# The first three groups on the window of the later ones: 168 keys per 64 tokens, one pair of bias tables, other loads

## The chip, the cores and the metric

One core of a Trainium2 chip runs one program. The metric is device microseconds of one execution; lower is better. PE is the matmul engine TensorE, DVE is VectorE, ACT is ScalarE, POOL is GpSimd; SP only issues transfers. Each engine works through its own queue in order and waits at an instruction until the semaphores of that instruction are there.

## What is computed

Attention with a local window and eight global keys, over 4 batches, 8 heads, 768 tokens and 64 features per head; its output is the input of a two-layer network with an ELU between the layers. The heart of the reference:

```python
keep = (pos[None, :] < n_global) | ((rel >= 0) & (rel < n_local))   # rel = query position - key position
scores = scale * q @ k.T - slopes * dist                            # dist = rel, or n_local for a far global key
a = softmax(where(keep, scores, -1e9))
x = (a @ v) as 3072 rows of 512
h = x @ w_in                                                        # 512 -> 2048
out = where(h > 0, h, exp(min(h, 0)) - 1) @ w_out                   # 2048 -> 512
```

Here `n_global` is 8 and `n_local` is 96. All sums are float32 or finer; `w_in` and `w_out` arrive as float64.

## The kernel before, in words

The 3072 tokens are 12 **groups** of 256 tokens (two tiles of 128). The network's hidden width is cut into 16 pieces, `fc` 0 to 15. A group needs, for each piece, the up product `h` (`mm1`, 12 matmuls of 256 columns: the high and low halves of the weight times the high part of x, then the high half times the low part `xl`), five elementwise steps, and the down product `o` (`mm2`, 6 matmuls of 512 columns). Each of the 32 weight pieces comes once, 512 KB of float64 bits (`bits`), and `weight` turns it into two fp32r halves: one ACT step, three to four DVE steps on `g`, one copy, and one subtraction on POOL.

Attention is done per group and pair of heads, so four **pairs** per group. The last nine groups use `far` and `turned`: 64 queries see 168 keys (96 before, 32, the 8 global ones, 32), the probabilities are turned by DVE and two transfers through DRAM. The first three groups, twelve pairs, use `pair` and `heads32` instead, in plain float32: scores of 128 queries against 256 keys (`s`, one tile; the very first tile of the sequence has 128 keys only), bias and maximum on DVE (`L451`), exponent on ACT (`L453`), 1/sum on DVE, the division (`norm`) on any of three engines, four transposes per tile on PE (`t`), copies to SBUF (`pt`), and the product with the values (`pv`). `xh` and `xl` are the high and low part of the result. `rqv` holds queries and values of a pair and is loaded before `rk`, its keys.

The two kinds of attention have bias tables of their own: `tab0`/`tab1` (256 wide) are made in `setup`, `far0`/`far1` (168 wide) later by `face`, on POOL.

Nothing is ordered by hand. `Plan.add` collects every step with alternatives of engine, an assumed cost and a due time; `Plan.order` walks a list schedule over them, picks engine and buffer slot, and the instructions are written out in that order. The network's pieces of the first three groups go in four segments (`SEGS`): pieces 0 to 3 for groups 0, 1 and 2, then 4 to 7 for the three, and so on. Until the first up product `warm` puts filler matmuls (`none<-fill`, `L930`) where the plan sees PE idle. The buffers of the weight pieces 12 to 15 serve the first pairs (`FIRST`, `EARLY`), so these weights are loaded only after all pairs.

Of the kernel before, what the change touches and what calls it, by code (L numbers as in the profile page):

```python
# [34 lines left out]
KW = P + NT * (NG + P)  # L35
KS = BACKW + NT * KN
VC = 2 * NT * P

# [169 lines left out]
def pe(cols):  # L208
    return (("PE", cols * 0.47, False),)
# [37 lines left out]
class Kernel:  # L247
# [64 lines left out]
    def consts(self):  # L312
        self.ident = self.const("ident", [P, P])
        self.tab0, self.tab1 = self.const("tab0", [P, P]), self.const("tab1", [P, 2 * P])
# [7 lines left out]
    def setup(self):  # L322
# [20 lines left out]
        tab0, tab1 = self.tab0.t, self.tab1.t  # L343
        nnl = self.c.tile([P, 1], F32, name="nnl")
        ii = m.tile([P, 2 * P], I32, tag="io0", name="ii")
        d = m.tile([P, 2 * P], F32, tag="io1", name="d")
        j = self.c.tile([P, NG], I32, name="tabj")
        g = self.c.tile([P, NG], F32, name="tabg")
        after = m.tile([P, P], F32, tag="io2", name="after")

        nc.gpsimd.iota(ii[:, P:], pattern=[[-1, P]], base=0, channel_multiplier=1)
        nc.gpsimd.iota(ii[:, :P], pattern=[[-1, P]], base=NL, channel_multiplier=1)
# [11 lines left out]
        nc.vector.tensor_tensor(tab0, tab1[:, P:], d[:, P:], ALU.add)  # L364
        nc.vector.tensor_scalar(g, g, nnl, None, ALU.add)
        nc.vector.tensor_copy(tab1[:, P:], tab0)
        nc.vector.tensor_tensor(tab0[:, :NG], tab0[:, :NG], g, ALU.max)
        nc.vector.tensor_tensor(tab1[:, :NL], tab1[:, :NL], d[:, :NL], ALU.add)
        nc.vector.tensor_copy(tab1[:, NL:P], g)
        self.g = g  # L370


    def weight(self, which, fc, due, after):
# [20 lines left out]
        p.add(act(DM) + pool(DM, False), lambda e: self.copy(e, w.t[:, HI], gf()), [g], [w], due - 3000)  # L394
# [16 lines left out]
    def pair(self, b, gi, hp, xh, xl, due, step, X):  # L411
        nc, p = self.nc, self.plan
        t0 = gi * NT
        nq, nk = W, KW
        rqv = self.sb("rqv", "rqv", [P, nq + VC], slots=X.get("rqv"))
        rk = self.sb("rk", "rk", [P, nk], slots=X.get("rk"))
# [9 lines left out]
        p.add(act(W) + dve(W, True) + (("POOL", 60 + 1.1 * W, True),), lambda e: self.scaled(e, q32()[:, 0], q32()[:, 0], sc), [rqv], [rqv], due - 9000)  # L426
        pv = self.bank("pv", "pv", [P, NT, P], X.get("pv"))
        for tiles in (range(NT),) if X.get("whole") else ((i,) for i in range(NT)):
            self.heads32(b, hp, t0, tiles, q32, k32, v32, rqv, rk, pv, due - 2 * step, 2 * step, X)
# [3 lines left out]
        if "pr" in X:  # L433
            self.held += [o for v in (rqv, rk) for o in v.readers]
# [8 lines left out]
    def softmax(self, b, h, t, s, m, pr, st, i, d):  # L443

        nc, p = self.nc, self.plan
        lo = 0 if t else P
        n = 2 * P - lo
        at = (b * self.H + h) * (self.S // P) + t
        nm = self.nmax.t[:, at:at + 1]
        tab = self.tab1.t if t else self.tab0.t  # L450
# [19 lines left out]
    def heads32(self, b, hp, t0, tiles, q32, k32, v32, rqv, rk, pv, due, step, X):  # L470
# [6 lines left out]
        n = {i: 2 * P - lo[i] for i in tiles}  # L477
        pts = {}

        def scores(e):  # L480
            for m, i in enumerate(tiles):
                c0 = NG + i * (NG + P) + lo[i]
                for r, s in zip(rows, ss):
# [672 lines left out]
```

## Time and profile before

| what | us |
|---|---|
| median of 3 runs | 660.91 (660.63 to 661.07) |
| the profiled execution | 661.28 |
| its span, first to last instruction | 659.4 |

The profiled execution lies 0.37 above the median, and 1.88 of it lie outside the span. A row of the timeline gives start, duration, engine, line, operation, output and inputs, and in brackets the idle time ahead of it with what ended it. Durations of neighbours on DVE and ACT overlap by some hundredths to a tenth of a microsecond; on PE the next start tells more than the duration.

### The profile page before, as it was taken

To read this page: it belongs to the slowest core of one execution; us is meant where nothing else is said; L and a number is where in the kernel's file an instruction comes from. 1 tells how busy PE (TensorE), PEld (TensorE's weight loads), DVE (VectorE), ACT (ScalarE), POOL (GpSimd) and SP (SyncE) were. 2 spreads that over 40 slices of the span, in tenths; PEclk is the share of its full clock that TensorE was granted. 3 is DMA by queue.
4 is the path that set the end of the run, shared out by engine and by line. 5 is a ranking of instruction groups with operands and counts; after the bars stand their busy time and mean duration, and the time that the engine had idled before them with its cause. 6 is when DMAs were issued, how large, how long until landed. Compare 5 with 4: busy or idle time off the path is not lost.

```text
span 659.4 us, 15420 instructions
## 1 busy us (share of the span) xinstructions
PE 647.1 (98%) x5584; PEld 564.0 (86%) x5584; DVE 386.2 (59%) x1287; ACT 403.4 (61%) x1209; POOL 150.1 (23%) x420
## 2 busy tenths in 40 slices
PE   8989999999999999999999999999999999999996
PEld 5767788898888888889889889889888888888995
DVE  6999879888664563563553554564554454443232
ACT  6999867665654664664664665655565565554442
POOL 3665654554220220220210111121121121110000
PEclk9999999999999999999999999999999999999999
DMA  7994273200263452462453354344245264030001
GB/s 306 401 407 158 80 279 98 55 2 1 70 196 101 121 148 82 120 166 83 120 140 108 107 134 128 96 128 136 71 142 142 65 163 132 34 96 1 34 1 34
DMA packets 67185, 80.55 MB, mean 122 GB/s; under 512 B 6048, under 2 KB 49312, under 8 KB 67104
## 3 DMA queue, kind: packets, MB, share of 16 engines
q1 hardware_dynamic: 66816, 79.39, 38.7%
q8 instruction: 45, 0.74, 0.5%
q14 instruction: 36, 0.29, 0.2%
q10 hardware_dynamic: 288, 0.13, 0.1%
HBM read 59.05 MB, written 20.45 MB: 121 GB/s over the span
## 4 chain that ended last, share of the span: by engine, by line
PE 83%; DVE 5%; DMA 4%; ACT 3%; issue 2%; POOL 1%; SPq 1%; POOLq 0%; DVEq 0%; ACTq 0%
PE o L752 37%; PE h L730 37%; PE pv L616 4%; PE s L544 3%; DMA bits<-in_w_out_dram 1%; DMA rqv<-in_qkv_dram 1%; DVE g L390 1%; DMA bits<-in_w_in_dram 1%; DMA pt<-dd 1%; PE t L512 1%; DVE g L388 1%; PE pv L490 1%; POOL w L309 1%; DVE g L392 1%; PE s L484 0%
## 5 line engine op out<-in xcount | busy, mean ns | idle before, releaser
L730 PEld LDWEIGHTS h<-xh,w 128*128 128x128 f32 x1536 | 233.6, 188 | 31.2 <-issue 1.1
L752 PE MATMUL o<-w,gh 128*128 128x512 f32 x768 | 243.5, 400 | 1.2 <-ACT gh L301 1.1
L730 PE MATMUL h<-xh,w 128*128 128x256 f32 x1536 | 243.6, 282 | 0.3 <-DVE gl L309 0.2
L738 DVE SCALAR_TENSOR_TENSOR h<-e,h 128x256 f32<-128x256 f32 x192 | 82.0, 427 | 175.1 <-ACT e L737 174.9
L752 PEld LDWEIGHTS o<-w,gh 128*128 128x128 f32 x768 | 129.9, 189 | 25.7 <-ACT gh L301 5.5
L736 ACT ACTIVATE e<-h 128x256 f32<-128x256 f32 x192 | 73.9, 385 | 125.0 <-PE h L730 124.5
L580 POOL TENSOR_SCALAR pr<-pr,st 128x168 f32<-128x168 f32 x144 | 58.3, 405 | 368.4 <-DVE st L461 248.1
L752 PE MATMUL o<-w,gl 128*128 128x512 f32 x384 | 128.0, 396 | 0.0
L730 PE MATMUL h<-xl,w 128*128 128x256 f32 x768 | 120.7, 279 | 0.1
L301 ACT CAST gh<-h 128x256 fp32r<-128x256 f32 x192 | 71.4, 372 | 67.0 <-DVE h L738 65.4
L309 DVE TENSOR_TENSOR gl<-h,gh 128x256 fp32r<-128x256 f32 x192 | 80.2, 418 | 45.7 <-ACT gh L301 45.4
L730 PEld LDWEIGHTS h<-xl,w 128*128 128x128 f32 x768 | 102.8, 188 | 0.5 <-DVE xl L309 0.3
L737 ACT ACTIVATE e<-e 128x256 f32<-128x256 f32 x192 | 79.9, 416 | 4.6
L572 ACT ACTIVATE pr<-pr,nmax 128x168 f32<-128x168 f32 x144 | 61.5, 427 | 20.4 <-DVE nmax L570 20.4
L752 PEld LDWEIGHTS o<-w,gl 128*128 128x128 f32 x384 | 61.8, 188 | 2.8 <-issue 0.8
L585 DVE STREAM_TRANSPOSE tr<-pr 128x192 f32<-128x192 f32 x144 | 48.0, 360 | 1.8 <-POOL pr L580 0.6
L309 POOL TENSOR_TENSOR w<-g,w 128x512 fp32r<-128x512 f32 x32 | 42.8, 1346 | 20.7 <-ACT w L301 17.8
L570 DVE CUSTOM_DVE_ANT_0 pr<-s,far 128x168 f32<-128x168 f32 x144 | 39.2, 327 | 11.9 <-PE s L544 11.9
L616 PEld LDWEIGHTS pv<-pt,v 64*64 64x64 f32 x1152 | 27.5, 133 | 8.7 <-PE h L730 5.8
L616 PE MATMUL pv<-pt,v 64*64 64x64 f32 (+1 forms) x1152 | 32.4, 250 | 0.2 <-DMA pt<-dd 0.2
L309 DVE TENSOR_TENSOR xl<-pv,xh 128x256 fp32r<-128x256 f32 x48 | 20.3, 423 | 17.1 <-ACT xh L301 15.9
L544 PE MATMUL s<-qk 64*64 64x168 f32 x576 | 27.3, 304 | 0.0
(101 smaller groups left out, 518.7 us busy)
## 6 DMA issues: line engine op xcount, KB each, us to landing
dd<-tr SPq DMA_DIRECT2D x72, 192.0 KB, 2.8
qk<-in_qkv_dram SPq DMA_DIRECT2D x36, 312.0 KB, 3.1
v<-in_qkv_dram SPq DMA_DIRECT2D x36, 256.0 KB, 3.5
pt<-dd SPq DMA_DIRECT2D x72, 128.0 KB, 2.9
bits<-in_w_in_dram SPq DMA_DIRECT2D x16, 512.0 KB, 8.0
bits<-in_w_out_dram SPq DMA_DIRECT2D x16, 512.0 KB, 8.8
out_dram<-ob SPq DMA_DIRECT2D x23, 256.0 KB, 2.1
rqv<-in_qkv_dram SPq DMA_DIRECT2D x12, 384.0 KB, 6.6
```

The source lines that it names most:

```text
L301: self.nc.scalar.copy(out, x)
L309: self.on(e).tensor_tensor(out, x, y, ALU.subtract)
L544: nc.tensor.matmul(ss[j].t[r * HW:(r + 1) * HW, i, :LW], q()[g, i * P + r * HW:i * P + (r + 1) * HW], k()[g, i * KN + r * HW:i * KN + r * ...
L572: p.add(act(LW, extra=200), lambda e, pr=pr, i=i, j=j, nm=nm: nc.scalar.activation(pr.t[:, :LW], pr.t[:, :LW], AF.Exp, bias=nm, scale=-1.0 ...
L580: nc.gpsimd.tensor_scalar(pr.t[:, :LW], pr.t[:, :LW], st.t[:, n, 3:4], 1.0, ALU.mult, ALU.mult)
L585: nc.vector.transpose(tr.t[:, :, j, i], pr.t.rearrange("p (b r) -> p b r", r=32))
L616: self.nc.tensor.matmul(pv[g].t[j * 64:j * 64 + 64, i].rearrange("p (q r) -> p q r", q=4)[:, q], vv[rows, 2 * i + a, j], pt.t[rows, q, a, ...
L730: nc.tensor.matmul(h.t, w1.t[:, s, cc * P:(cc + 1) * P], x.t[:, cc], start=n == 0 and cc == 0, stop=n == 2 and cc == self.NCC - 1)
L736: p.add(act(W, True), lambda e: nc.scalar.activation(ex.t, h.t, AF.Relu, scale=-1.0), [h], [ex], d - 8000)
L737: p.add(act(W), lambda e: nc.scalar.activation(ex.t, ex.t, AF.Exp, scale=-1.0), [ex], [ex], d - 8000)
L738: p.add(dve(W), lambda e: nc.vector.scalar_tensor_tensor(h.t, ex.t, -1.0, h.t, ALU.add, ALU.max), [h, ex], [h], d - 8000)
L752: nc.tensor.matmul(acc[i].t, g.t[:, i * P:(i + 1) * P], w2.t[:, s], start=fc == f0 and n == 0 and s == HI, stop=fc == f1 - 1 and n == 1)
```

## The change

`pair` and `heads32` use the layout of the later groups: per tile eight small score matmuls (two halves of 64 queries, two heads, 168 keys) through a function that `far` now shares, one 168-wide bias, exponent and division per head and tile, transposes of two pieces of 84 keys, and value products of 84 keys by 64 queries, twice as many and half as wide. `face` and the 256-wide tables go; `far0` and `far1` are made in `setup`, where ACT now copies three times. A pair loads `qk` (312 KB) and then `v` (84 partitions of 4 KB, 336 KB). Three numbers of the plan change too (assumed matmul cost, the spacing `NEXT` of the pairs of groups 1 and 2, the slot lists), and the high half of a weight may be copied by DVE.

```diff
-KW = P + NT * (NG + P)
+CW = LW // 2
+VN = 4 * NT * P
...
-    return (("PE", cols * 0.47, False),)
+    return (("PE", cols * 0.458, False),)
...
+        nc.scalar.copy(far0, far1)
...
+        nc.vector.tensor_tensor(far1, far1, d, ALU.add)
+        for r, at in halves:
+            nc.scalar.copy(far1[r, at:at + NG], g[r])
...
-        p.add(act(DM) + pool(DM, False), lambda e: self.copy(e, w.t[:, HI], gf()), [g], [w], due - 3000)
+        p.add(act(DM) + pool(DM, False) + dve(DM, True), lambda e: self.copy(e, w.t[:, HI], gf()), [g], [w], due - 3000)
...
-        loads = [p.add(sp(), lambda e: nc.sync.dma_start(rqv.t, src[:, :nq + VC]), writes=[rqv], due=due - 9000, nbytes=P * (nq + VC) * 4)]
-        loads += [p.add(sp(), lambda e: nc.sync.dma_start(rk.t, src[:, nq + VC:]), writes=[rk], due=due - 9000, nbytes=P * nk * 4)]
+        loads = [p.add(sp(), lambda e: nc.sync.dma_start(qk.t, src[:, :W + KS]), writes=[qk], due=due - 9000, nbytes=P * (W + KS) * 4)]
+        loads += [p.add(sp(), lambda e: nc.sync.dma_start(v.t[:CW], src[:CW, W + KS:]), writes=[v], due=due - 9000, nbytes=CW * VN * 4)]
...
+    def scores(self, qk, ss, tiles):
+        q, k = qk.t[:, :W], qk.t[:, W:]
+        for m, i in enumerate(tiles):
+            for r in range(2):
+                for j in range(2):
+                    g = slice(j * HW, (j + 1) * HW)
+                    self.nc.tensor.matmul(ss[j].t[r * HW:(r + 1) * HW, m, :LW], q[g, i * P + r * HW:i * P + (r + 1) * HW],
+                                          k[g, i * KN + r * HW:i * KN + r * HW + LW], start=True, stop=True)
...
-                for a in range(lo[i] // P, 2):
-                    for j in range(2):
-                        nc.tensor.matmul(pv.t[rows[j], i], v32()[:, 2 * i + a, j], pts[i].t[:, j, a], start=a == lo[i] // P, stop=a == 1)
+                for r in range(2):
+                    x = slice(r * HW, (r + 1) * HW)
+                    for a in range(2):
+                        for j in range(2):
+                            nc.tensor.matmul(pv.t[rows[j], i, x], vv[:CW, i, r, a, j], pts[i].t[:CW, j, a, x], start=a == 0, stop=a == 1)
...
-                        nc.tensor.transpose(tp.t[:, j, a], prs[j].t[:, a * P:(a + 1) * P], self.ident.t)
+                        nc.tensor.transpose(tp.t[:CW, j, a], prs[j].t[:, a * CW:(a + 1) * CW], self.ident.t)
...
-    def face(self, due):
...
-    NEXT = 8000.0
+    NEXT = 6000.0
```

How the queues move is seen at two places. The first is the head of ACT's queue. `rqv_153` and `qk_158` are the queries of the first pair, `far_70` and `far_71` are `far0` and `far1`, `tabg` holds the bias of the global keys. Before:

```order
L231 DMA n_raw<-in_n_dram 128x4
L331 ACT_TABLE_LOAD
L331 ACTIVATE act<-act 128x1
L437 ACTIVATE rqv_153<-rqv_153,scale 128x256
L453 ACTIVATE pr_195,st_74<-pr_195,nmax 128x128
```

And with the change:

```order
L232 DMA n_raw<-in_n_dram 128x4
L332 ACT_TABLE_LOAD
L332 ACTIVATE act<-act 128x1
L361 COPY far_70<-far_71 128x168
L377 COPY far_71<-tabg 64x8 x2
L440 ACTIVATE qk_158<-qk_158,scale 128x256
L455 ACTIVATE pr_204,st_74<-pr_204,nmax 128x168
```

The scaling of the first queries now stands behind table copies, the last of which need the finished tables of DVE.

The second place is PE where the last of the twelve pairs ends and group 2 begins. `pv_1269` and `pv_1368` are the last value products, `h_1298` and `h_1403` the first up product of group 2, an `o` a down product (`gh` and `gl` are its inputs). Before:

```order
L490 MATMUL pv_1269<-pt_1229,rqv_761 64x128 x4
L490 MATMUL pv_1269<-pt_1249,rqv_761 64x128 x4
L730 MATMUL h_1298<-xh_1005,w_78_338 128x256 x8
L730 MATMUL h_1298<-xl_1017,w_78_338 128x256 x4
L730 MATMUL h_1322<-xh_1005,w_84_447 128x256 x8
L730 MATMUL h_1322<-xl_1017,w_84_447 128x256 x4
L752 MATMUL o_1370<-w_81_580,gh_1361 128x512 x2
```

With the change:

```order
L497 MATMUL pv_1368<-pt_1327,v_833 64x64 x8
L497 MATMUL pv_1368<-pt_1355,v_833 64x64 x8
L700 MATMUL o_1248<-w_93_1064,gh_1339 128x512 x2
L700 MATMUL o_1305<-w_93_1064,gh_1339 128x512 x2
L678 MATMUL h_1403<-xh_1086,w_78_498 128x256 x8
L678 MATMUL h_1403<-xl_1096,w_78_498 128x256 x4
L700 MATMUL o_1248<-w_93_1064,gl_1346 128x512
L700 MATMUL o_1305<-w_93_1064,gl_1346 128x512
L700 MATMUL o_1248<-w_99_1174,gh_1399 128x512 x2
L678 MATMUL h_1442<-xh_1086,w_84_594 128x256 x4
```

Two pieces of group 1's down product, twelve matmuls, that stood ahead of the last pair now stand behind it, between the up products of group 2. The eight score matmuls of the first `far` pair, ahead of it too, also moved behind. Ahead of the last bias instruction of the twelve pairs, DVE's queue holds 21 `L390`/`L392` and 16 `L387`/`L388` steps on weights before, and 18 and 12 with the change, plus 4 copies of high halves; 13 divisions and query scalings stand there in both, ten of the divisions 256 wide before and 168 now; 14 elementwise steps of the network before, 10 now; 9 `pt` copies of 256 and 5 of 128 columns before, 14 of 256 now.

## Rows read from the trace of the kernel before

**Rows 1.** The page, part 1: busy us (share of the span), instructions.

```profile
PE 647.1 (98%) x5584; PEld 564.0 (86%) x5584; DVE 386.2 (59%) x1287; ACT 403.4 (61%) x1209; POOL 150.1 (23%) x420
```

**Rows 2.** Stretches: length; PE, PEld, DVE, ACT, POOL busy; clock; DMA share; GB/s.

```profile
15.00:20.00 5.00, 5.00 (x37) 3.03 (x34) 4.70 (x22) 4.81 (x16) 3.32 (x6) 1.00 1.03 401
50.00:60.00 10.00, 9.60 (x83) 7.28 (x82) 9.93 (x33) 9.00 (x29) 4.64 (x6) 1.00 0.59 217
80.00:90.00 10.00, 8.78 (x58) 7.81 (x57) 7.25 (x20) 6.65 (x19) 6.10 (x12) 1.00 1.00 372
```

**Rows 3.** Timeline of PE: first scores, first up product, end of the pairs.

```profile
6.73 0.93 PE L484 MATMUL s<-rk,rqv 64*128 64x128 f32 x8 [0.41 <-ACT rqv L437]
...
28.65 1.64 PE L730 MATMUL h<-xh,w 128*128 128x256 f32 x12
...
78.25 1.56 PE L730 MATMUL h<-xh,w 128*128 128x256 f32 x8
...
80.48 1.11 PE L730 MATMUL h<-xh,w 128*128 128x256 f32 x8
...
83.19 1.21 PE L752 MATMUL o<-w,gh 128*128 128x512 f32 x4 [1.13 <-ACT gh L301]
```

**Rows 4.** Timeline of DVE and ACT: constants, first scaling, first and last bias.

```profile
5.63 0.17 DVE L239 CAST n_f<-n_raw 128x4 f32<-128x4 int32 x1 [1.02 <-DMA n_raw<-in_n_dram]
...
7.89 0.29 DVE L451 CUSTOM_DVE_ANT_0 pr<-s,tab 128x128 f32<-128x128 f32 x1
...
70.33 0.42 DVE L451 CUSTOM_DVE_ANT_0 pr<-s,tab 128x256 f32<-128x256 f32 x1
...
6.15 0.51 ACT L437 ACTIVATE rqv<-rqv,scale 128x256 f32<-128x256 f32 x1 [3.39 <-DMA rqv<-in_qkv_dram]
```

**Rows 5.** DVE groups by shape, 0 to 80 us: busy us, mean ns.

```profile
L451 DVE CUSTOM_DVE_ANT_0 pr<-s,tab 128x256 f32<-128x256 f32 x40 | 15.9, 415 | 1.5 <-PE t L512 1.4
L390 DVE SCALAR_TENSOR_TENSOR g<-bits,g 128x512 int32<-128x512 int32 x12 | 8.3, 700 | 0.0
L388 DVE TENSOR_SCALAR g<-g 128x512 int32<-128x512 int32 x13 | 6.5, 518 | 0.0
...
L451 DVE CUSTOM_DVE_ANT_0 pr<-s,tab 128x128 f32<-128x128 f32 x8 | 2.2, 280 | 0.0
...
L570 DVE CUSTOM_DVE_ANT_0 pr<-s,far 128x168 f32<-128x168 f32 x4 | 1.1, 330 | 0.7 <-PE s L544 0.7
```

**Rows 6.** Timeline of PE: a first-group pair, then a `far` visit.

```profile
45.29 1.13 PE L484 MATMUL s<-rk,rqv 64*128 64x256 f32 x8
46.35 1.09 PE L490 MATMUL pv<-pt,rqv 128*64 128x128 f32 x16
47.38 0.74 PE L730 MATMUL h<-xh,w 128*128 128x256 f32 x4
...
108.33 0.90 PE L616 MATMUL pv<-pt,v 64*64 64x128 f32 x32
109.05 0.75 PE L544 MATMUL s<-qk 64*64 64x168 f32 x16
109.73 0.50 PE L752 MATMUL o<-w,gl 128*128 128x512 f32 x1
```

**Rows 7.** Chain that ended last: start us, us, what.

```profile
144.06 0.94 PE h L730 x8
145.00 1.17 PE o L752 x5
```

**Rows 8.** Loads of the page, part 6: KB each, median us to landing.

```profile
rqv<-in_qkv_dram SPq DMA_DIRECT2D x12, 384.0 KB, 6.6
...
rk<-in_qkv_dram SPq DMA_DIRECT2D x12, 200.0 KB, 6.6
```

**Rows 9.** Last weight of pieces 4 to 7: its low half, its first use.

```profile
97.19 1.30 POOL L309 TENSOR_TENSOR w<-g,w 128x512 fp32r<-128x512 f32 x1 [2.13 <-ACT w L301]
...
101.50 0.62 PE L752 MATMUL o<-w,gh 128*128 128x512 f32 x2
```

More of the change, by code (lines that the diff above doesn't have):

```diff
@@ L433, in pair @@
         if "pr" in X:
-            self.held += [o for v in (rqv, rk) for o in v.readers]
+            self.held += qk.readers + v.readers
     def scaled(self, e, out, x, sc):
@@ L463, in inverse, with norm, heads32 @@
         self.plan.add((("DVE", 290.0, False),), inverse, [st], [st], due, slack=slack)
-    def norm(self, pr, lo, st, i, due, both):
-        n = 2 * P - lo
-        return self.plan.add((act(n, extra=90) if both else ()) + (("DVE", 130 + 0.53 * n, True), ("POOL", 60 + 1.1 * n, True)), lambda e: self.scaled(
-            e, pr.t[:, lo:], pr.t[:, lo:], st.t[:, i, 3:4]), [pr, st], [pr], due)
-    def heads32(self, b, hp, t0, tiles, q32, k32, v32, rqv, rk, pv, due, step, X):
+    def norm(self, pr, st, i, due):
+        return self.plan.add(act(LW, extra=90) + (("DVE", 130 + 0.53 * LW, True), ("POOL", 60 + 1.1 * LW, True)), lambda e: self.scaled(
+            e, pr.t, pr.t, st.t[:, i, 3:4]), [pr, st], [pr], due)
+    def heads32(self, b, hp, t0, tiles, qk, v, pv, due, step, X):
         nc, p = self.nc, self.plan
@@ L533, in far @@
         p.add(sp(), lambda e: nc.sync.dma_start(v.t, src[:, W + KS:]), writes=[v], due=due - 13500, nbytes=P * VC * 4)
-        q, k = lambda: qk.t[:, :W], lambda: qk.t[:, W:]
         sc = self.scale.t[:, hp:hp + 1]
-        p.add(act(W) + dve(W, True) + (("POOL", 60 + 1.1 * W, True),), lambda e: self.scaled(e, q(), q(), sc), [qk], [qk], due - 8000, slack=self.LOADED)
+        p.add(act(W) + dve(W, True) + (("POOL", 60 + 1.1 * W, True),), lambda e: self.scaled(e, qk.t[:, :W], qk.t[:, :W], sc), [qk], [qk], due - 8000, slack=self.LOADED)
         ss = [self.bank("s", "s", [P, NT, 2 * P]) for _ in range(2)]
-        def scores(e):
-            for i in range(NT):
-                for r in range(2):
-                    for j in range(2):
-                        g = slice(j * HW, (j + 1) * HW)
-                        nc.tensor.matmul(ss[j].t[r * HW:(r + 1) * HW, i, :LW], q()[g, i * P + r * HW:i * P + (r + 1) * HW],
-                                         k()[g, i * KN + r * HW:i * KN + r * HW + LW], start=True, stop=True)
         rest = []
@@ L550, in chain @@
             rest.append(self.turned(b, hp, gi * NT, ss, due, end, X))
-        return scores, [qk], ss, chain, (rest, v, hp, xh, xl, end)
+        return lambda e: self.scores(qk, ss, range(NT)), [qk], ss, chain, (rest, v, hp, xh, xl, end)
     def turned(self, b, hp, t0, ss, due, end, X):
```

162 lines of the change are left out of this document (55 added, 107 removed).

## The prediction

> **What bounds the kernel now.** First the page: PE is busy 647.1 of 659.4 us [rows 1]. A busy PE is no proof of a full PE, so the second view is the stretches. From 15 to 20 us DVE is busy 4.70 of 5 and ACT 4.81, the loads run at 401 GB/s, and the 5.00 of PE are filled up with warming matmuls; from 50 to 60 us DVE is busy 9.93 of 10 and PE 9.60 [rows 2]. The timeline then says where PE becomes the pace-maker: first scores at 6.73, first useful up product at 28.65, and after the last pair PE starts group 2 at 78.25 [rows 3]. So there are two regimes. Until about 78 us DVE and ACT set the pace, PE follows. After it PE runs the network, a piece at 12 x 0.118 us up and 6 x 0.234 us down [rows 7], and whatever comes sooner at 78 us comes sooner at the end, as long as the weights keep up. The change touches only the first regime, so it is worth what it moves there, no more than a few microseconds of 660.
>
> **The start.** ACT scaled the first queries at 6.15, as they landed; the first bias of DVE ran at 7.89, because DVE had constants to make after the scalars of the masks came in at 5.63 [rows 4]. Now ACT stands behind the copies of the global columns, which need DVE's finished tables. DVE has about as many constant steps as before and is done near 7.6, if the scalars land as before. Two copies of 8 columns cost ACT some 0.2 us each (the small cast on DVE took 0.17 [rows 4]), so the scaling starts near 8.0 in place of 6.15. The old distance from scaling to scores was 0.58 us [rows 3, 4]; half a scores step of the narrow kind is 0.34 [rows 6]. The first bias comes near 9.1, 1.2 us later. What is queued behind ACT's copies is the whole chain of pair 0; PE fills with warming matmuls, and DVE idles. I take 1.2 in full; if later slack swallows it, it is 0.
>
> **DVE until the last bias.** Before, the last of 48 bias steps starts at 70.33 [rows 4]. The order says what stands ahead of it, the rows what one costs.
>
> - Biases: 40 of 256 columns at 0.415 and 8 of 128 at 0.280 are 18.8 us; 48 of 168 at 0.330 [rows 5] are 15.8: 3.0 less.
> - Divisions: ten shrink from 256 to 168 columns, by the same 0.085 each at most; one query scaling (0.415) more: 0.4 less.
> - Copies of transposed probabilities: 9 of 256 and 5 of 128 columns become 14 of 256. Priced as biases of that width, 0.7 more. One more result copy, 0.4 more.
> - Network steps: 14 become 10, at 0.415 (256 columns): 1.7 less. Not saved, only moved behind.
> - Weight steps: 21 to 18 at 0.70 and 16 to 12 at 0.518 [rows 5]: 4.2 less, again only moved. Four copies of high halves come to DVE. No row has them on DVE; 512 columns lie between 0.415 (a step of 256) and 0.70, I take 0.518: 2.1 more.
>
> Sum: 3.0 + 0.4 - 0.7 - 0.4 + 1.7 + 4.2 - 2.1 = 6.1 us less. With the start, the last bias comes 6.1 - 1.2 = 4.9 us sooner, at 65.4. ACT, the other full engine, gets the same relief, since every exponent narrows as its bias does.
>
> **PE until then.** Per pair the scores took 1.06 us (45.29 to 46.35) and the values 1.03 (to 47.38); the narrow scores, of the same form as the `far` ones, take 0.68 [rows 6]: 0.38 less. Values have no row: 16 matmuls of 64 columns over 84 keys, two column halves side by side. From below: as many columns stream as before, 1.03. From above: the `far` values, also 32 loads of 64 columns, took 0.72 with four quadrants side by side [rows 6]; with two, at most 1.44. I take 1.1, nearest to the row with the same columns, halves and engine state. From 28.65, which I leave where it is (the start's 1.2 against group 0's lighter steps), to 78.25 PE has 49.6 us; it now needs 3.5 less (moved pieces, below) and 8 x 0.3 less for the eight pairs of groups 1 and 2: 43.7 us. It is given 49.6 - 4.9 = 44.7. It fits, narrowly, so DVE still decides. Group 0's pairs run under filler, where PE time costs nothing.
>
> The Trainium skill ("TensorE: Matmul & The Clock Gate", LDWEIGHTS) speaks against the values: loading weights costs their columns over 1.2 GHz whatever the depth, 53 ns for 64 columns, an estimate of 1.7 us for 32 loads. The `far` row shows 32 such loads within 0.72 us, so here the rule in its serial reading does not hold across quadrants; for two halves no run here shows it. By it the pairs would cost PE 5 us more, and the end would come out near 662.
>
> **The end of the pairs and after.** Shift of the last pair's values: 4.9 us sooner, 73.4. But PE then still owes two down pieces, 12 x 0.234 = 2.8 us, and the `far` scores, 0.68, that were done ahead of this place before: 3.5 us. They pay in part for themselves: before, group 2's first twelve up products took 2.23 us (78.25 to 80.48) instead of 12 x 0.118 = 1.41, waiting for the last pair's result, and PE stood 1.13 us for the next `gh` [rows 3]. With two down pieces in hand these 1.9 us have cover. Net: 4.9 - 3.5 + 1.9 = 3.3 us.
>
> **What I cost at nothing.** POOL's tables for `far`: POOL is busy 23% [rows 1]; removing them frees an engine that nobody waits for long. The loads: 584 KB per pair before [rows 8], 648 now, 0.79 MB in all or 2.0 us at 401 GB/s, at the tail of the loading, where the last weights lie ready long before their use. The plan's cheaper matmul cost only reorders.
>
> So the span comes to 659.4 - 3.3 = 656.1, the execution to 658.0 with the 1.9 around it, and the median, which lies 0.4 below the profiled execution, to **657.6 us**.
>
> **Rivals.**
>
> *Holes go too* (655.2). PE was idle 0.4 of 10 us from 50 to 60 [rows 2], some 2.0 over the five such stretches from 28 to 78 if they are alike. Lighter DVE and ACT could close them, and a third of the 1.2 at the start be swallowed: 2.4 more. For it: DVE at 9.93 was the cause. Against: the pairs now stand denser between fewer network pieces.
>
> *PE becomes the bound through the values* (660.0). At 1.44 a pair instead of 1.1, PE needs 2.7 us more, 46.4 against 44.7 given, and with any idle time some 0.7 more is lost: 2.4 of the 3.3 go. For it: doubled loads. Against: the `far` row.
>
> *Weight preparation becomes the bound* (661.6). The moved steps, 1.7 + 4.2 = 5.9 us, have to be done on DVE after the pairs. Counting all work, DVE saves 3.0 + 0.4 - 0.7 - 0.4 = 2.3, and pays 2.1 for the copies and 1.2 for the start: it is 1.0 late. The last weight of pieces 4 to 7 was ready at 98.49 and first used at 101.50 [rows 9], 3.0 us of slack. If DVE is serial from 65 to 98 us, PE, 3.3 sooner, waits 3.3 + 1.0 - 3.0 = 1.3 there; if each later group of four pieces, where slack is no larger, waits too, until all of DVE's 1.0 shows, the result is 0.7 slower. It decides from 3.3 us of PE waits between 85 and 130 on. Against: DVE was busy only 7.25 of 10 from 80 to 90 [rows 2], so 5 us and more of its idle time lie there.
>
> *Loads set the pace* (664.5, the slower side). If the queues wait for data and not for DVE, the pairs end 2.0 us later, not 4.9 sooner, and 2.0 + 3.5 - 1.9 = 3.6 are lost. It turns the sign once waits for loads on DVE or ACT before 65 us add up to 3.3 us. For it: 401 GB/s at 15 to 20 us [rows 2]. Against: the loads of all pairs stand early in SP's order. "DMA: Bandwidth & Descriptors" of the Trainium skill (section on the semaphore's increment of 16) adds that a transfer runs on the largest number of up to 16 engines that divides its partitions, 14 for 84; no run here shows it; by it the added 2.0 would be an estimated 3.4.
>
> *Nothing moves* (660.9): start and denser pairs eat it all.
>
> **Chances and range.** Forecast 0.52; holes too 0.13; PE bound 0.11; weights bound 0.11; loads 0.08; nothing 0.05. A difference of 0.2% (1.3 us) is about what three runs can tell from none: faster means below 659.6, slower above 662.2. Faster takes the first two, a third of PE bound and a third of weights bound (where only the 1.3 us is paid): 0.73. Slower takes the loads and a fifth of the weights (where the copies cost 0.70): 0.10. Same: the rest, 0.17. The range goes from the holes' case, 655.0, to just above PE bound, 660.8, since the forecast's own (start 0 to 1.2, values 1.03 to 1.44, copies 0.415 to 0.70) runs from 656.4 to 659.
>
> **What would show it.** Right: first scores near 8.5 and not 6.7; bias steps of 0.33; the 48th near 65.4; scores of a pair at 0.68 and values at 1.0 to 1.2; group 2's first up product near 74.3 without the hole; from 130 us on the same pace, earlier by 3 us. Wrong: values at 1.4 or more; PE waits for `w` or `gl` between 80 and 130; waits of ACT, DVE or POOL for loads of more than a microsecond; idle DVE between 9 and 30 us.

## The result and the profile after

The changed kernel takes 668.75 us (median of 5 runs, 667.51 to 670.7), the kernel before 660.91: the ratio is 1.0115, 95% interval 1.0099 to 1.0131. The change costs 1.15%, where 0.5% of gain was forecast. The profiled execution took 667.51 us, its span is 665.7, 6.3 us longer than that of before.

The page, part 1, answers to [rows 1]: TensorE is as full as it was.

```profile
PE 649.9 (98%) x5891; PEld 567.9 (85%) x5891; DVE 382.5 (57%) x1286; ACT 399.6 (60%) x1207; POOL 148.7 (22%) x412
```

Stretches of the changed kernel, the columns those of [rows 2], with two more from the place where TensorE's clock fell:

```profile
15.00:20.00 5.00, 4.09 (x66) 2.80 (x65) 3.95 (x22) 3.00 (x13) 1.87 (x4) 1.00 1.03 307
25.00:30.00 5.00, 0.89 (x7) 0.41 (x8) 1.33 (x7) 4.33 (x14) 2.65 (x5) 0.78 0.99 360
30.00:35.00 5.00, 5.00 (x46) 3.57 (x46) 3.65 (x14) 3.90 (x15) 1.58 (x3) 0.54 0.98 379
50.00:60.00 10.00, 9.09 (x137) 7.28 (x137) 9.74 (x30) 8.26 (x29) 6.75 (x8) 1.00 1.02 351
80.00:90.00 10.00, 10.00 (x84) 8.93 (x78) 8.65 (x16) 7.07 (x17) 6.04 (x5) 1.00 0.67 246
```

The two stretches around TensorE's hole, in the kernel before:

```profile
25.00:30.00 5.00, 5.00 (x41) 3.61 (x40) 4.52 (x15) 4.68 (x17) 3.39 (x4) 1.00 1.04 396
30.00:35.00 5.00, 4.94 (x45) 3.93 (x44) 4.42 (x16) 5.00 (x18) 3.21 (x5) 1.00 1.04 409
```

From 15 to 20 us the DMA engines are as busy as before (share 1.03) and move 307 GB/s where they moved 401. From 50 to 60 us they are still full, 1.02, where before the share was down to 0.59. A full share is no full rate: here the packets took longer (their times stand with the first experiment). What came late is seen on ACT:

```profile
7.63 0.40 ACT L377 COPY far<-tabg 64x8 f32<-64x8 f32 x2 [2.48 <-DVE far L375]
8.06 0.51 ACT L440 ACTIVATE qk<-qk,scale 128x256 f32<-128x256 f32 x1
...
25.02 1.21 ACT L392 ACTIVATE g<-bits 128x512 f32<-128x512 f32 x2 [3.80 <-DMA bits<-in_w_out_dram]
26.13 0.42 ACT L455 ACTIVATE pr<-pr,nmax 128x168 f32<-128x168 f32 x1
```

ACT stands 3.80 us for two weights, and the exponents of the next pair (`L455`) wait behind them in its fixed order. On TensorE (the rows that answer to [rows 3], and a later pair for [rows 6]):

```profile
8.62 0.80 PE L465 MATMUL s<-qk 64*64 64x168 f32 x16 [1.01 <-ACT qk L440]
...
29.80 1.13 PE L497 MATMUL pv<-pt,v 84*64 84x64 f32 x16 [4.11 <-DVE xl L310]
...
35.80 1.20 PE L678 MATMUL h<-xh,w 128*128 128x256 f32 x8
...
59.05 0.80 PE L465 MATMUL s<-qk 64*64 64x168 f32 x16
59.78 1.15 PE L497 MATMUL pv<-pt,v 84*64 84x64 f32 x32
...
79.57 1.15 PE L497 MATMUL pv<-pt,v 84*64 84x64 f32 x32
80.65 1.19 PE L700 MATMUL o<-w,gh 128*128 128x512 f32 x4
81.68 1.11 PE L678 MATMUL h<-xh,w 128*128 128x256 f32 x8
82.62 0.63 PE L678 MATMUL h<-xl,w 128*128 128x256 f32 x4
83.09 0.63 PE L700 MATMUL o<-w,gl 128*128 128x512 f32 x2
```

TensorE stands 4.11 us, and in the two stretches around it the granted clock is 0.78 and 0.54 of 2.4 GHz; before it was 1.00 there. The wait is put down to `xl` of DVE at 29.32, but that one had itself waited for ACT (the row is below). The first up product runs 7.15 us later than in [rows 3], the first of group 2 at 81.68 and not 78.25.

On DVE the first bias and the 48th answer to [rows 4]; between them stand the two waits that came of ACT's stand:

```profile
9.19 0.33 DVE L453 CUSTOM_DVE_ANT_0 pr<-s,far 128x168 f32<-128x168 f32 x1 [1.26 <-PE s L465]
...
27.09 0.16 DVE L472 TENSOR_REDUCE st<-st 128x2 f32<-128x4 f32 x1 [2.54 <-ACT pr L455]
...
29.32 0.42 DVE L310 TENSOR_TENSOR xl<-pv,xh 128x256 fp32r<-128x256 f32 x1 [1.55 <-ACT xh L302]
...
71.69 0.33 DVE L453 CUSTOM_DVE_ANT_0 pr<-s,far 128x168 f32<-128x168 f32 x1
```

The loads of part 6 answer to [rows 8]. The line of `bits` had a median of 8.8 us before; that of `qk` counts the later groups' loads too, and the early `v` has no median on the page:

```profile
qk<-in_qkv_dram SPq DMA_DIRECT2D x48, 312.0 KB, 3.3
...
bits<-in_w_out_dram SPq DMA_DIRECT2D x16, 512.0 KB, 10.9
...
v<-in_qkv_dram SPq DMA_DIRECT2D x12, 336.0 KB
```

To see where the 6.3 us lie I count the 2304 up products in order of time and note when the 5%, the 20% and the last (99.9%) point start. Before: 81.31, 166.53, 648.61. After: 85.10, 170.74, 654.94. So 3.8 us are lost by the 5% point, 0.4 up to the 20% point, and **2.1 us more in the steady stretch behind it** (484.20 against 482.07), where the changed kernel's trace shows no wait of TensorE.

### The profile page after: what moved, and what is told of

It reads as the page before. It is cut to its first block, busy times and chain, and to the rows that moved or that the text cites. A ratio compares the mean times of both kernels' runs of the same rounds, so it can differ in the third digit from the quotient of the medians.

```text
span 665.7 us, 16043 instructions
## 1 busy us (share of the span) xinstructions
PE 649.9 (98%) x5891; PEld 567.9 (85%) x5891; DVE 382.5 (57%) x1286; ACT 399.6 (60%) x1207; POOL 148.7 (22%) x412
## 4 chain that ended last, share of the span: by engine, by line
PE 91%; DMA 5%; DVE 2%; issue 1%; ACT 0%; SPq 0%; DVEq 0%
PE o L700 41%; PE h L678 40%; PE pv L605 4%; PE s L465 3%; DMA qk<-in_qkv_dram 2%; DMA bits<-in_w_out_dram 2%; DMA v<-in_qkv_dram 1%; PE pv L497 1%; PE t L518 1%; DVE g L399 1%; DVE g L397 0%; DVE pr L453 0%; DVE gl L310 0%; DVE g L395 0%; ACT g L392 0%
## 5 line engine op out<-in xcount | busy, mean ns | idle before, releaser
L678 PE MATMUL h<-xl,w 128*128 128x256 f32 x768 | 123.2, 283 | 0.0
L678 PEld LDWEIGHTS h<-xl,w 128*128 128x128 f32 x768 | 105.2, 188 | 0.1
L455 ACT ACTIVATE pr<-pr,nmax 128x168 f32<-128x168 f32 x192 | 82.1, 428 | 21.9 <-DVE nmax L453 21.7
L453 DVE CUSTOM_DVE_ANT_0 pr<-s,far 128x168 f32<-128x168 f32 x192 | 53.3, 326 | 13.9 <-PE s L465 13.3
L465 PE MATMUL s<-qk 64*64 64x168 f32 x768 | 38.4, 311 | 1.0 <-ACT qk L440 1.0
L455 ACT ACTIVATION_READ_ACCUMULATOR pr<-pr,nmax 128x1 f32 x192 | 36.3, 189 | 0.0
L605 PE MATMUL pv<-pt,v 64*64 64x128 f32 (+1 forms) x1152 | 32.3, 250 | 0.0
```

The costliest lines, as they stand in the source:

```text
L453: first = p.add((("DVE", 85 + 1.042 * LW, False),), lambda e: nc.vector.tensor_tensor_reduce(x(), s.t[:, i, :LW], tab, -(2.0 ** -(h + 1)), ...
L455: p.add(act(LW, extra=200), lambda e: nc.scalar.activation(x(), x(), AF.Exp, bias=nm, scale=-1.0, accum_out=st.t[:, n, 0:1]), [pr], [pr, s ...
L465: self.nc.tensor.matmul(ss[j].t[r * HW:(r + 1) * HW, m, :LW], q[g, i * P + r * HW:i * P + (r + 1) * HW], k[g, i * KN + r * HW:i * KN + r * ...
L605: self.nc.tensor.matmul(pv[g].t[j * 64:j * 64 + 64, i].rearrange("p (q r) -> p q r", q=4)[:, q], vv[rows, 2 * i + a, j], pt.t[rows, q, a, ...
L678: nc.tensor.matmul(h.t, w1.t[:, s, cc * P:(cc + 1) * P], x.t[:, cc], start=n == 0 and cc == 0, stop=n == 2 and cc == self.NCC - 1)
```

## The experiments

All are edits of the changed kernel unless the kernel before is named; every ratio is to the kernel before, timed beside that run. The diffs are cut to what was changed. "5%" and "steady" are the two measures just given, read from the profiled execution of each run.

### The early loads

**Whole rows.** e1_v128:

```diff
-nc.sync.dma_start(v.t[:CW], src[:CW, W + KS:])
+nc.sync.dma_start(v.t, src[:, W + KS:])
```

> The changed kernel with one edit: each of the 12 early v loads fetches all 128 rows of 4 KB (512 KB, the last 44 rows zeros that nobody reads) in place of 84 rows (336 KB); the order of all instructions is the same. Theory (places in SBUF): a load lasts as long as its bytes per partition make it, so 84 rows of 4 KB already last as long as 128. Then 2.1 MB more cost nothing: the time stays within 2 us of the changed kernel's 668.75, the rate at 15 to 20 us rises from 307 to about 400 GB/s, and a 4 KB packet takes about 162 ns there and not about 240. Rival 1 (bytes alone): 12 x 176 KB at 401 GB/s are 5.4 us more, 674. Rival 2 (engines): 84 rows use 14 of 16 engines; 512 KB on 16 engines take 1.31 us, 336 KB on 14 take 0.98, so 12 loads cost 4 us more, about 672. Rival 3 (the start or the plan's numbers, not the loads): again bytes, 668 to 674, with packets as slow as before the edit.

Measured: 664.62 us, ratio 1.0058 (1.0045 to 1.0071). It loads 2.1 MB more and is 4.1 us faster. Rate and packets came as the first theory said, the time fell below what it allowed. Its stretches:

```profile
15.00:20.00 5.00, 4.67 (x71) 3.34 (x71) 4.62 (x23) 3.58 (x16) 1.46 (x4) 1.00 1.02 400
25.00:30.00 5.00, 2.58 (x36) 1.94 (x36) 3.12 (x14) 4.55 (x15) 2.26 (x3) 0.80 1.03 404
```

In the trace's DMA packets the median of those of 4 KB, from 15 to 25 us, is 164 ns before, 234 in the changed kernel and 162 here. Loads that the edit does not touch were slowed too: packets of 2496 bytes, the rows of `qk`, take 124 ns in the changed kernel and 100 here (median from 5 to 25 us). ACT's stand for the weights shrinks from 3.80 to 2.22 us, the first up product comes at 32.82, the 5% point at 81.90. Bytes alone are refuted, with rival 3, and so is rival 2's rate, by which this run would have been the slower one.

**Another number of rows, and whole rows in halves.** e2_v80_4 and, on the kernel before, e4_rqv64:

```diff
+(nc.sync.dma_start(v.t[:80], src[:80, W + KS:]), nc.sync.dma_start(v.t[80:CW], src[80:CW, W + KS:]))
```

```diff
-nc.sync.dma_start(rqv.t, src[:, :nq + VC])
+[nc.sync.dma_start(rqv.t[r], src[r, :nq + VC]) for r in (slice(0, 64), slice(64, 128))]
```

> The changed kernel with each early v load cut into two, rows 0 to 79 and rows 80 to 83, one behind the other; the same bytes, the same order. Theory (places in SBUF): nothing changes but some 12 more issues on SP, 668 to 670; 4 KB packets still take about 240 ns around 20 us. Rival 2 (engines that divide the rows): 80 rows run on all 16 engines, 0.82 us against 0.98 for 84 rows on 14; the four rows run on 4 engines beside other loads; so up to 12 x 0.16 = 2 us come back, 666 to 667, and if the odd 84 itself is what slows the packets, all 7 us come back, 661.

> The kernel before the change with one edit: each early load of 384 KB (queries and values, 128 rows) is cut into two of 64 rows, one behind the other; same bytes, same rows, same engines as 64 is divided by 16. Theory (places in SBUF): each half lands on half of the places, so a pair's load lasts up to twice as long, 0.96 us more at 401 GB/s, 12 of them up to 11.5 us of the queues' time; the rate at 15 to 20 us falls well below 401 GB/s, and the time is 664 to 672. Rival 1 (bytes) and rival 2 (engines): no change, 660.9 +- 0.6 (12 more issues on SP of some 0.35 us each).

Measured: e2 670.81, 1.0155 (1.0141 to 1.017); 4 KB packets 286 ns, those of `qk` 165. Both theories fell: it is slower than the changed kernel, and so are its packets. e4 669.84, 1.0131 (1.0116 to 1.0146), as the first theory said. One stretch of each, e2 first:

```profile
15.00:20.00 5.00, 2.98 (x55) 2.09 (x50) 2.09 (x11) 2.05 (x10) 2.35 (x5) 1.00 1.04 244
```

```profile
20.00:25.00 5.00, 3.15 (x16) 1.49 (x16) 2.29 (x11) 2.98 (x10) 3.10 (x5) 1.00 1.04 259
```

Two loads of 64 rows, same bytes, make before 8.8 us slower: its first up product moves from 28.65 to 34.39. This prices the disputed thing by itself: what counts, for rows of this size, is how many of them a load covers at once. The 12 more issues that come with the halves do not explain it: with a DMA share of 1.04 the DMA engines had work all the time. The Trainium skill ("SBUF — State Buffer", Door 1) says that 128 rows share 16 ports, eight to a port, and that rows 0 to 63 reach eight of them; the rate of e4 from 20 to 25 us, 259 GB/s where before it was 398, agrees in direction, and no run here shows the ports themselves. By that map, as an estimate, 84 rows of 4 KB take as long as 128, no longer, and e1 shows them longer: the map can explain a slow rate, but not this.

**Half of the data.** e3_vhalf loads 84 rows of 2 KB, e10_v128half 128 rows of 2 KB; both multiply the second tile's values with the first tile's:

```diff
+nc.sync.dma_start(v.t[:CW, :VN // 2], src[:CW, W + KS:W + KS + VN // 2])   # e3
+nc.sync.dma_start(v.t[:, :VN // 2], src[:, W + KS:W + KS + VN // 2])       # e10
...
-nc.tensor.matmul(pv.t[rows[j], i, x], vv[:CW, i, r, a, j], ...)
+nc.tensor.matmul(pv.t[rows[j], i, x], vv[:CW, 0, r, a, j], ...)
```

> The changed kernel with half of each early v load: 84 rows of 2 KB (168 KB); the second tile's values are multiplied with the first tile's, so the second tile of the first three groups is left out of what is computed, while every instruction but the 12 loads is the same. Theory (loads set the pace): bytes per partition of a pair are 2496 + 2048 = 4544, 128 less than before the change (4672), so the stall of ACT near 25 us and PE's hole of 4.1 us near 30 us go, the first up product runs near 29 us (35.80 in the changed kernel, 28.65 before the change), and the time is 656 to 659, as forecast without the loads. Rival 3 (start, plan numbers, or PE's values): the loss stays, 666 to 669. In between: what is left above 657 is not the loads'.

> The changed kernel with early v loads of 128 rows of 2 KB (256 KB, 44 rows of zeros); the second tile's values are multiplied with the first tile's, so the second tile of the first three groups is left out of what is computed; every other instruction is the same. A pair then brings 568 KB in whole loads, 16 less than before the change: the loads cost what the forecast assumed. If the forecast's other steps hold (queue of bias adds 6 us shorter, hole of 1.9 us covered, 3.3 us gained by the 80th us), the 5% point of the up products (81.31 before) comes at 78 to 79 and the time is 659.5 to 660.5 with the steady stretch's 2.1 us as it is. If the loads were not the only loss ahead of 80 us, it stays at 80 or later: 661 to 662.5, and a wait on ACT, DVE or TensorE that is not for a load must stand in it.

Measured: 661.9, 1.0014 (1.0003 to 1.0026), and 662.71, 1.0022 (1.0013 to 1.0031). The 5% points are 80.27 and 80.25: with the loads at 330 to 340 GB/s up to 20 us (e3) or at 390 to 410 (e10) the same, so the loads no longer decide. The first up product runs at 29.64 in e10, the 48th bias at 66.83, the last pair's values end at 75.87. Both are slower than forecast for them. In e3's forecast the 2.1 us of the steady stretch (484.20) were missing. e10's had them; its 5% point was to come at 78 to 79. Ahead of that point e10's trace has a fall of TensorE's clock, in stretches of a microsecond (PE busy, clock, DMA share, GB/s):

```profile
37.00:38.00 1.00, 0.43 (x4) 1.00 0.96 381
38.00:39.00 1.00, 0.52 (x4) 1.00 1.00 393
39.00:40.00 1.00, 0.35 (x10) 1.00 1.02 397
40.00:41.00 1.00, 1.00 (x32) 0.72 1.02 418
41.00:42.00 1.00, 1.00 (x17) 0.50 1.00 404
42.00:43.00 1.00, 1.00 (x11) 0.50 1.04 410
43.00:44.00 1.00, 1.00 (x5) 0.58 1.05 426
```

After three microseconds in which TensorE was busy 1.30, the clock falls from 2.4 to 1.2 GHz; the four rows of it sum to 1.7 us of lost work (0.28 + 0.50 + 0.50 + 0.42). How much of it reaches the end is not shown. The shortest of e10's twelve runs is 1.64 us under its profiled execution (661.37 to 663.01) and may lack the fall.

**The planner is told.** e11_v128_told, on top of e1:

```diff
-nbytes=CW * VN * 4
+nbytes=P * VN * 4
```

> Whole early v loads of 128 rows (as the run at 664.62), and the planner is told their 512 KB in place of 336, so that it puts the weights' first step on ACT where the data will be there. Theory (ACT's fixed order turns a late load into a hole on TensorE): ACT's stand of 2.2 us for weights near 25 us shrinks, the hole on TensorE of 2.4 us and its drop to 0.80 of the clock at 25 to 30 us go, and 2 to 3 us come back: 661.5 to 663. Rival (the data are late in any order): 664.6 +- 0.7, the stand goes elsewhere.

Measured: 664.21, 1.0051 (1.0038 to 1.0064): the rival, nearly. The stand of ACT is gone, the first up product runs at 28.20, sooner than before, the 3% point at 60.99 in place of 67.00, and yet the 5% point only from 81.90 to 81.48. From 50 to 70 us DVE is full (9.72 and 9.94 of 10), so that the products gained early wait for the pairs all the same; that DVE is the whole reason was not tested. TensorE's hole and the fall of its clock are gone too (1.00 in every stretch), so all three together, and what else the new order moved, were worth 0.42 us at the 5% point:

```profile
25.00:30.00 5.00, 4.92 (x66) 3.90 (x67) 4.91 (x18) 4.65 (x16) 1.43 (x4) 1.00 1.02 404
...
60.00:70.00 10.00, 9.70 (x106) 8.01 (x105) 9.94 (x36) 9.69 (x35) 4.55 (x5) 1.00 0.49 184
```

**The start.** e12_v128_start, on top of e1:

```diff
-nc.scalar.copy(far1[r, at:at + NG], g[r])
+nc.vector.tensor_copy(far1[r, at:at + NG], g[r])
```

> Whole early v loads of 128 rows, and the two small copies at the end of the tables are made by DVE and not by ACT, so that ACT's first query scaling no longer stands behind the tables. Theory (the start's 1.2 us lie on the path): the first scores come 1 to 1.5 us sooner than 8.6 us and 0.5 to 1.2 us of it reach the end: 663.4 to 664.1. Rival (the loads set the pace from 10 us on and swallow it): 664.6 +- 0.5.

Measured: 665.85, 1.0089 (1.0065 to 1.0112). The scores start at 7.01 (8.52 in e1), the first bias at 8.17 (9.09), and the 5% point is 82.17, no sooner. With the loads of e1 the start's 1.2 us do not reach the end; with the loads out of the way, as in e10, that was not tried.

**The plan's numbers.** e6_oldplan:

```diff
-    return (("PE", cols * 0.458, False),)
+    return (("PE", cols * 0.47, False),)
-        p.add(act(DM) + pool(DM, False) + dve(DM, True), ...
+        p.add(act(DM) + pool(DM, False), ...
-    NEXT = 6000.0
+    NEXT = 8000.0
```

> The changed kernel with the planner's three numbers of before: 0.47 ns a column and not 0.458, groups 6000 to 8000 us apart as before (NEXT 8000), and the rounded weights on ACT or GpSimd alone. The loads are the changed kernel's. Theory (loads): the queues still run at 250 to 320 GB/s up to 25 us and ACT still stands for weights, so the time stays at 667 to 670. Rival (plan numbers): weights and pairs come in before's order, the hole on TensorE near 30 us goes, 661 to 663. A middle value would say that the order decides which engine pays for the late loads.

Measured: 672.05, 1.0155 (1.0133 to 1.0177): worse than the changed kernel, above both ranges. The numbers of before don't cure it: the loads are as slow (316 GB/s from 15 to 20 us, 274 to 25), and ACT stands 2.33 and 1.96 us for weights. What makes it slower still was not tested. Steady: 484.20.

**Another layout.** e7_relay (the load; the transposes become one of 128 keys and two of 64 per head):

```diff
-VN = 4 * NT * P
+VN = 3 * NT * P
-nc.tensor.transpose(tp.t[:CW, j, a], prs[j].t[:, a * CW:(a + 1) * CW], self.ident.t)
+nc.tensor.transpose(tp.t[:, j, 0], prs[j].t[:, :P], self.ident.t)
+nc.tensor.matmul(tp.t[r, j, 1], prs[j].t[r, LW - HW:], self.ident.t[r], start=True, stop=True)
```

> The changed kernel with the early values laid out on all 128 rows: of the 168 keys of 64 queries the first 128 stand on 128 rows and the last 40 of both halves on rows 24 to 63 and 88 to 127 (zeros between); 3 KB a row, 384 KB a load in place of 336 KB on 84 rows; what is computed and the order are unchanged, the transposes of a tile are six small ones in place of four. Theory (places in SBUF): although 48 KB more are loaded, rate and packets are those of whole loads (about 400 GB/s, 162 ns), and a row takes 1 KB less than with whole loads of 512 KB, so the 664.62 measured there fall by up to 12 x 128 KB at 401 GB/s = 3.9 us; half of it on the path gives 662 to 664, and the first up product comes before 32.8 us. Rival 1 (bytes alone): 0.6 MB more cost 1.4 us, 670. Rival 2 (it was the zeros or the order that helped whole loads): no gain on 664.6.

Measured: 677.38, 1.0237 (1.0215 to 1.0259). The rate is as expected, 396 to 411 GB/s from 5 to 30 us, but the layout puts more work on TensorE, from 8 to 82 us (busy us, mean ns):

```profile
L521 PE MATMUL t<-ident,pr 64*64 64x128 f32 x176 | 19.2, 295 | 0.0
L519 PE MATMUL t<-ident,pr 128*128 128x128 f32 x44 | 14.0, 319 | 1.7 <-ACT pt L302 1.7
```

That is 33.2 us in place of 15.4 for the changed kernel's transposes there, and the run ends above all three forecasts. That this work is the whole loss is likely and was not tested; the run says nothing on the loads' share of the end.

### The steady stretch

No wait of over 0.2 us stands there; the products themselves start further apart. Means of the distance from one start to the next, where the next is of the same kind, 170 to 645 us: those with `xl` 115.0 ns before, 119.0 after; those with `xh` 118.5 and 117.0; `o` with `gl` 229.5 and 232.7. All the runs above that come from the changed kernel have 119 and 484.2 to 484.6; e4, from before, has 115.1 and 481.75.

e5_place and e9_wplace (both of the changed kernel) and e8_before_place move tiles by multiples of 512 bytes:

```diff
+m.tile([P, 512], F32, tag="pad", name="pad")
```

(384 elements in e8; in e9 a constant of 384 ahead of the others, which moves weights and tiles alike.)

> The changed kernel with one unused tile of 2 KB per partition ahead of all working tiles: every working tile moves up 2048 bytes in SBUF, the weights stay; order, loads and arithmetic are the same. What it tests: from its 20% point to its end the changed kernel's up products take 484.20 us where those of before take 482.08, without any wait on TensorE there; its products with the rest xl start 119 ns apart, those of before 115, and the tiles xh, xl, gl lie elsewhere against the weights in the two kernels. Theory (the place of the moving tile against the weights sets the spacing): by the spacings seen at each distance, xl goes back to about 115 ns, some 900 products x 4 ns = 3 us or a little more, and the time is 664.8 to 666.5; the loss ahead of 70 us stays as it is. Rival (the order of far visits among the products, from the plan's numbers): nothing moves, 668.75 +- 0.7.

> The kernel before the change with one unused tile of 1.5 KB per partition ahead of all working tiles (2 KB don't fit); nothing else differs. Theory (place): by the spacings that the two traces show at each distance, about half of the products with xl go from 115 ns to near 120 and those with xh move by up to 2 ns; the steady stretch gets 1 to 2.5 us longer, 661.9 to 663.5, with no new wait on TensorE. Rival (order or plan): 660.9 +- 0.4.

> The changed kernel with one unused constant of 1.5 KB per partition ahead of the others, so that weights and working tiles all move up 1536 bytes and the first weights stand at the address that they have in the kernel before; nothing else differs. Theory (the place of the weights sets the spacing of the products): those with xl go from 119 ns back to about 115, the steady stretch from 484.2 back to about 482 us, and the time is 666 to 667. Rival (something else that the two kernels differ in, such as the order or the stream of instructions): 668.75 +- 0.7 and 119 ns. That the working tiles' place alone does nothing is shown already (2 KB more there: 119.0 ns).

Measured: e5 668.38, 1.0097 (1.0077 to 1.0117), 119.0 ns; e8 661.26, 0.9999 (0.9982 to 1.0015), 115.1 ns; e9 668.66, 1.0126 (1.011 to 1.0141), 119.0 ns. The theory fell in this form three times. What stayed the same in each was the place to within 256 bytes: `xh` and `xl` at 128 in before, at 64 in every variant of the changed kernel (but for one early tile of `xh`, at 192 in both), the weights at 192 in all. The next five runs have pads of 64 or 128 bytes (e15 on top of e11, e16 and e17 on the kernel before):

```diff
+m.tile([P, 16], F32, tag="pad", name="pad")
+self.const("pad", [P, 16])
```

The first line is in e13 and e16, and with 32 elements in e15 and e17; the second, ahead of the constants, in e14 and e15.

> The changed kernel with one unused tile of 64 bytes per partition ahead of the working tiles: xh and xl then begin 128 bytes into a block of 256, as in the kernel before (64 in the changed kernel and in every variant of it so far; shifts by 2048 and by 1536 bytes kept that, and kept 119 ns); the weights stay at 192. Theory (the place to within 256 bytes sets the products' pace): the spacing of those with xl goes from 119 to 115 ns, of those with xh from 117 to 118.5, the stretch from the 20% to the last up product from 484.2 to 482.1, the time to 666.5. Rival (something else in the two programs): 119 ns, 668.7 +- 0.7.

> The changed kernel with 64 unused bytes ahead of the constants: weights move from 192 to 0 (mod 256), working tiles from 64 to 128, so that the distance between them stays that of the changed kernel and only the places themselves change. If the distance counts, xl stays at 119 ns and the steady stretch at 484.2; if the place of the working tiles alone counts, 115 ns and 482.1; if both places count on their own, a third value.

> Whole early v loads of 128 rows, the planner told of them (the run at 664.21), weights at 0 and working tiles at 0 (mod 256). If rows that begin on whole blocks are read fastest, the products with xl and xh come at 115 ns or less and the steady stretch under 482: 661.5 or less, and with 113 ns throughout near 658. If only 192 and 128 is a good pair, 664.2 +- 0.7.

> The kernel before the change with 64 unused bytes ahead of its working tiles: x goes from 128 to 192 (mod 256), the weights stay at 192; nothing else differs. Theory (place to within 256 bytes): the spacing of the xl products leaves 115 ns, by 1 to 4 ns in either direction, and the steady stretch of 482.1 moves by 1 to 3 us, without a wait on TensorE. Rival: 115 ns, 661.0 +- 0.4.

> The kernel before the change with 128 unused bytes ahead of its working tiles: the distance from the weights to xh and xl, mod 256, becomes 64, the one of the four that no run has shown (192: xl 115.0, xh 118.5 ns; 128: 119.0, 117.0; 0: 118.9, 118.3, each in two kernels or more). Theory (the distance alone sets the pace): the pair of spacings is a fourth one; on the evidence of the three it lies between 115 and 119 for xl and 117 and 118.5 for xh, the steady stretch between 480 and 486 us, the time between 658.9 and 664.9. If it is under 481.5, this kernel beats both. Rival (only 192 is good): the stretch takes 484 to 486, 663 to 665.

Measured, with the distance, the place of `xl` less that of the weights, mod 256 bytes:

| run | distance | ratio (interval) | xl ns | xh ns | steady us |
|---|---|---|---|---|---|
| before | 192 | 1 | 115.0 | 118.5 | 482.07 |
| e13 | 192 | 1.0063 (1.0047 to 1.0078) | 115.0 | 118.6 | 481.95 |
| changed | 128 | 1.0115 (1.0099 to 1.0131) | 119.0 | 117.0 | 484.20 |
| e14 | 128 | 1.008 (1.0065 to 1.0095) | 119.0 | 117.0 | 484.19 |
| e15 | 0 | 1.0071 (1.0055 to 1.0086) | 118.9 | 118.4 | 486.02 |
| e16 | 0 | 1.0081 (1.0062 to 1.01) | 118.9 | 118.2 | 485.88 |
| e17 | 64 | 1.0078 (1.0055 to 1.01) | 117.8 | 118.6 | 485.27 |

The distance sets the pace, not the place: e14 moved both and kept 119.0; e15 and e16, two different programs at distance 0, agree to 0.2 us. This rests on the last three columns. The ratios hold more than the distance: with the same 484.2 us they run from 1.008 (e14) to 1.0126 (e9), and in e17's profiled execution TensorE stands still from 43 to 45 us, so that its 5% point comes at 84.17 and not 81.31. Sixty-four unused bytes on the kernel before (e16) cost it 0.8%, 3.8 us of that in the steady stretch. The view by groups shows it too, if less sharply, as mean ns of one product, first the changed kernel, then e13:

```profile
L678 PE MATMUL h<-xh,w 128*128 128x256 f32 x1200 | 190.0, 280 | 0.0
L678 PE MATMUL h<-xl,w 128*128 128x256 f32 x597 | 95.5, 282 | 0.0
```

```profile
L679 PE MATMUL h<-xh,w 128*128 128x256 f32 x1204 | 191.4, 281 | 0.0
L679 PE MATMUL h<-xl,w 128*128 128x256 f32 x601 | 93.9, 279 | 0.0
```

**Both treated.** e18_told_m64 is e11 with e13's pad.

> The changed kernel with both losses treated as far as the runs allow: whole early v loads of 128 rows of which the planner is told (664.21 alone), and the working tiles 64 bytes further, at before's distance of 192 (mod 256) from the weights. If the two losses are separate and add, the steady stretch takes 482.0 us and not 484.6, products with xl start 115 ns apart, and the time is 661.4 to 662.4, within measurement of before (660.9). If they are not separate, the time stays above 663.

Measured: 660.9 us, ratio 1.0 (0.9988 to 1.0012): 5% point 81.99, steady 481.76, `xl` 115.0 ns. The two losses are separate and add: the pad takes 2.9 us off the steady stretch of e11, 2.25 off that of the changed kernel. Not all of the first loss is gone; in e10 the 5% point stands at 80.25. No version beat the kernel before.

## Why the prediction was wrong

Point by point:

- *The start*: right in size (first bias forecast 9.1, came at 9.19), wrong in weight. I took 1.2 us in full; e12 took it away from e1 and the end did not move.
- *DVE's queue*: right in its work, not in its waits. Forecast 6.1 us less work ahead of the 48th bias; the rows of DVE between the first and the 48th bias sum to 72.8 us before and 66.8 after. But DVE's idle time there rose from 3.9 to 9.3, so the 48th bias came at 71.69 and not 65.4. With the loads out of the way (e10) it came at 66.83, 1.4 late.
- *TensorE's pairs*: right. Scores forecast 0.68, 0.73 from start to start; values forecast 1.1, 1.08. The serial price that the Trainium skill ("TensorE: Matmul & The Clock Gate", LDWEIGHTS) would give, an estimated 1.7 us, did not show.
- *End of the pairs*: right behind the last values, not ahead of them. The moved down pieces stand at 80.65, and group 2's first twelve up products take 1.41 us (81.68 to 83.09) without the hole; from the end of the last values to the 5% point it is 4.38 us, 1.4 more than before, where the forecast has 3.5 - 1.9 = 1.6. But the last values end 9.0 us after the 48th bias, before 8.0; the forecast moved both by the same 4.9. In e10 the values end 2.45 us sooner than before, and 2.45 + 1.9 - 3.5 = 0.85; its 5% point came 1.06 sooner.
- ***What I cost at nothing* is the step that failed**, in two entries. *The loads*: I priced 0.79 MB at 401 GB/s and put them at the tail. The price did not hold for these loads: with 84 rows of 4 KB in every second load what was in flight slowed, to 317 GB/s from 5 to 10 us (411 before) and 267 from 20 to 25, so not the tail but the weights of 25 us came late, and ACT, DVE and TensorE stood. Two of the prediction's own signs of being wrong are what came: a wait of ACT for loads of 3.80 us, and idle DVE (busy 1.33 of 5 from 25 to 30 us). The way to the end is the pairs' chain, as far as the 48th bias on DVE: from there to the 5% point it is 13.4 us in the changed kernel, in e1 and in e10, while the bias itself stands at 71.69, 68.48 and 66.83. ACT's stand and TensorE's clock catch the eye but are not the price; e11, in an order of its own, did without them and was 0.42 us sooner than e1. Measured by the 5% point, with e10 for the kernel without the loss: 85.10 - 80.25 = 4.85 us from the loads, of which 3.2 go when the same loads are made whole (e1), although that adds bytes, and the other 1.65 when those whole rows are halved.
- The second entry is *nothing*: I had no term for the steady stretch at all ("from 130 us on the same pace"). New and vanished tiles moved the working tiles by 64 bytes against the weights: 2.1 us.

The parts add up to the difference of the spans, 6.3: 4.85 (loads) - 1.06 (what the rest of the change gained, by e10) + 0.42 (5% to 20%, no cause sought) + 2.13 (steady) = 6.34 us. Against the forecast's span of 656.1 it is 9.6 us: these 4.85, 0.42 and 2.13, and 2.24 that the other steps stay short of their 3.3 even in e10, 1.4 at the 48th bias and 0.85 behind it. The rival *Loads set the pace* named the right resource and 664.5; it is 4.2 us too low, since it let the rate stand at 401 and knew nothing of the steady stretch. The rule cited there from the Trainium skill ("DMA: Bandwidth & Descriptors"), 14 engines for 84 rows, does not account for it: by it the whole rows of e1 would be slower than 84, and they are faster, and 80 rows and 4 would be no slower, and they are (e2). How many engines a load used no run here shows.

Open: why 84 rows of 4 KB are slower than 128 with more bytes, why a distance of 192 is the best of the four that I tried, and why e13 gains 3.8 us where its steady stretch gives 2.25 (0.48 more are ahead of the 5% point and 0.25 from there to the 20% point; the rest is not seen in the profiled executions, nor are the 2.1 us by which e14's median is below that of the changed kernel).

## What to carry to other kernels

Price a load by the rows that it covers and the bytes of one row, not by its bytes alone: here loads of 64, 80 and 84 rows of 3 to 4 KB also slowed what was in flight beside them, and a DMA share of 1.0 did not show that, only GB/s did. When a stretch without waits changes its pace, look at the distance between the matmul's two operands before looking for a cause in the order. Before you price a stand that catches the eye, take it away: here ACT's stand of 2.22 us, TensorE's hole and the fall of its clock went in e11 and 0.42 us came back, while in runs of one order the last bias of the pairs, on DVE, told the loss to a tenth of a microsecond.

## What was not expected of the hardware

- A 128-row load of 512 KB is cheaper than an 84-row load of 336 KB: 4 KB packets at 162 ns against 234, and 4.1 us less for the whole kernel although twelve such loads bring 2.1 MB more.
- The same matmuls, no waits, 64 or 128 unused bytes: 481.7 to 486.0 us for one stretch, by the distance of the moving tile from the weights.
- In e10 TensorE, busy 1.30 us from 37 to 40, fell from 2.4 to 1.2 GHz between 40 and 44 us, fully busy again, and lost 1.7 us of its clock. Not all of such a fall reaches the end: e18 has one of that size (0.67 from 40 to 45 us) and e11, the same program but for 64 unused bytes, has none; at the 5% point e18 is 0.5 us later.
